# The idle products of TensorE's front: half as many, each over 256 columns instead of 128

## The chip, the cores and the metric

The kernel runs on one core of a Trainium2 chip. The metric is device time in microseconds (us), and a smaller one is better. The engines have short names in the profile: PE is TensorE's matrix products, PEld its loads of the stationary operand (they overlap the products), DVE is VectorE, ACT ScalarE, POOL GpSimd, and SP SyncE, which here issues DMAs. Each engine works through a queue of its own in program order. A product of 32-bit floats stands in the records as two passes, each with its own load, so that one matmul in the code is two PE and two PEld records.

## The reference

A gated linear recurrence over 768 steps for 4 x 8 heads of width 48, and behind it a feed-forward layer with a squared ReLU over 3072 tokens:

```python
for t in range(S):
    new_re = ar * S_re - ai * S_im          # ar, ai: a_re, a_im at step t, magnitude limited to 0.999
    new_im = ar * S_im + ai * S_re
    S_re, S_im = new_re + k[t] (x) v[t], new_im
    y[t] = einsum('bhd,bhde->bhe', q[t], S_re)
x = y as (B*S, H*D)                          # 3072 x 384
h = np.maximum(x @ w_in, 0.0)                # 384 x 2048
return h * h @ w_out                         # 2048 x 384
```

The idle products have no part in this: their result is read by nothing.

## The kernel before

The tokens are cut into 24 chunks of 128, taken two at a time as a group, and there are 12 groups. For each chunk the recurrence becomes products: DVE and ACT make operands from the gates (`make_operands`: squares, inverse roots, running products `totals`, `carries`, `carried`, then four `products` with queries and keys, and `heads_moved`, L990, which shifts some heads with a product on PE). `chunk` then holds the work on scores: `scores` (L1050, and L1033 for the state of the chunk before), `masked` (DVE), `sums_of_values` (L1087), `tokens` (ACT, L1099), `added` (L1112). The feed-forward part is `first_product` (L1179 for the chunks of the first two groups, one chunk at a time; L1195 for later groups, 256 tokens at a time), `squared_relu` on ACT, and the second product (L1215, and L1285 for most groups). `move_gaps` (L1169, L1170, and the ACT copy L1164) moves tokens between rows for the first chunk.

The weights come as 64-bit floats and are decoded in the kernel: a DMA brings a block as `words`, ACT makes two partial words (`low_part` L682, `high_part` L690) and DVE joins them (`decode`, L698). There are 16 such blocks. This decoding and the operands of the first groups fill DVE and ACT in the first 80 us, so TensorE has little to do there.

In that front TensorE runs idle products: `keep_busy` multiplies the identity `ident` with itself into a PSUM tile that nobody reads. The order of all work is written out by hand as a list of tokens, `FRONT`; each token `I<n>` calls `keep_busy(n)` once. The tokens I0 to I39 and I100 to I115 and two calls inside `scores` for the second chunk of the first group (L1040) make 58 calls. What they do:

```python
ident = const.tile([P, P], F32, name="ident")
idle = po.tile([P, DM], F32, tag="o", name="idle")[:, 0:P]
def keep_busy(n):
    for _ in range(2):
        nc.tensor.matmul(idle, lhsT=ident, rhs=ident, start=True, stop=True)
```

The idle products wait only for `ident` (POOL), and nothing waits for them but what stands behind them on PE's queue. In PE's order they stand at five places: 36 ahead of L630 (a transpose of the mask), 66 between L630 and the first L990, 2 inside the first chunk's block of scores work, 8 behind the first feed-forward products (L1179), and 4 inside the second chunk's scores.

## Time and profile before

| | before |
|---|---|
| median of 3 runs | 646.1 us (646.0 to 649.09) |
| the profiled execution | 644.23 us |
| its span, first to last instruction | 642.5 us |
| PE busy | 627.3 us, 98% of the span |
| DVE busy, ACT busy | 486.0 us (76%), 431.3 us (67%) |
| mean granted TensorE clock | 0.993 of full speed |

The span is 1.73 us shorter than the time of its own execution. PE is busy nearly throughout; where a change at the front is concerned, the questions are how early PE's unbroken work begins and whether it stays unbroken. The timeline rows give start and duration in us, engine, line, operation, output<-input, the number of instructions merged into the row, and in brackets the idle time before it with what ended it. A row's duration reaches to the modelled end of its last pass, so the pace of passes is read from one row's start to the next row's start.

### The profile page before, as it was taken

The numbers are of one execution on the slowest core, as the hardware profiler recorded it, in microseconds if no ns is written. First come the engines' busy times: TensorE is split into PE (matmuls) and PEld (weight loads), VectorE is DVE, ScalarE is ACT, GpSimd is POOL, SyncE is SP. The second block draws the span as 40 slices with busy tenths as digits, with TensorE's granted clock in tenths as the row PEclk, the third lists the DMA queues.
The fourth block names the chain that finished last, engine by engine and source line by source line (L and its number), as shares of the span: only waits on it lengthen the run. The fifth ranks groups of instructions, "written<-read, shape, count | busy, mean of one in ns | idle before, by whom it ended". The sixth has DMA issues, their size and how long they took to land.

```text
span 642.5 us, 16051 instructions
## 1 busy us (share of the span) xinstructions
PE 627.3 (98%) x6567; PEld 565.0 (88%) x6567; DVE 486.0 (76%) x975; ACT 431.3 (67%) x852; POOL 55.0 (9%) x124
## 2 busy tenths in 40 slices
PE   7989999999999999999999999999999999999996
PEld 7978878777899989999899999999989989999996
DVE  7969989978999865886888968878949859763130
ACT  5969989839696577685486577488587568544430
POOL 5430113001000011000110000100100011000000
PEclk9979999999999999999999999999999999999999
DMA  8996676071620723340731720823741741221201
GB/s 187 194 164 129 221 198 136 11 130 53 117 39 27 137 52 98 82 93 14 152 65 34 135 64 10 158 63 86 168 101 36 145 125 26 68 64 52 68 14 27
DMA packets 41494, 60.09 MB, mean 94 GB/s; under 512 B 5928, under 2 KB 29832, under 8 KB 41416
## 3 DMA queue, kind: packets, MB, share of 16 engines
q1 hardware_dynamic: 39240, 55.02, 39.2%
q0 software_dynamic: 1888, 3.69, 3.1%
q8 instruction: 52, 0.85, 0.6%
q10 hardware_dynamic: 288, 0.32, 0.2%
q14 instruction: 26, 0.21, 0.1%
HBM read 48.76 MB, written 4.72 MB: 83 GB/s over the span
## 4 chain that ended last, share of the span: by engine, by line
PE 94%; ACT 3%; DVE 1%; issue 1%; DMA 1%; POOL 0%; SPq 0%; ACTq 0%; POOLq 0%; DVEq 0%
PE h_ps L1195 32%; PE o_ps L1285 29%; PE o_ps L1215 6%; PE a_ps L1050 5%; PE h_ps L1179 5%; PE idle L579 4%; PE y L1033 3%; PE y L1087 3%; PE turns L1060 3%; PE turns L1112 3%; PE o_ps L990 1%; ACT part L682 1%; ACT part L690 1%; DMA last<-qk 1%; ACT h L1185 0%
## 5 line engine op out<-in xcount | busy, mean ns | idle before, releaser
L1195 PE MATMUL h_ps<-x,w 128*128 128x256 f32 x960 | 211.4, 379 | 0.0
L1195 PEld LDWEIGHTS h_ps<-x,w 128*128 128x128 f32 x960 | 181.4, 190 | 23.8
L1285 PE MATMUL o_ps<-w,h 128*128 128x192 f32 x640 | 109.8, 327 | 0.0
L1202 ACT ACTIVATE h<-h_ps 128x512 f32<-128x512 f32 x80 | 47.5, 594 | 86.2 <-PE h_ps L1195 86.0
L1285 PEld LDWEIGHTS o_ps<-w,h 128*128 128x128 f32 x640 | 103.9, 190 | 1.2 <-ACT o L1144 0.4
L499 DVE TENSOR_TENSOR pr<-ab 128x384 f32<-128x384 f32 (+3 forms) x196 | 70.7, 378 | 5.5 <-ACT ab L905 1.3
L1285 PE MATMUL o_ps<-w_sum,mix 128*128 128x192 f32 x320 | 55.2, 328 | 0.0
L499 DVE TENSOR_TENSOR ab<-pr 128x48 f32<-128x48 f32 (+3 forms) x210 | 50.1, 261 | 5.3
L1203 ACT ACTIVATE h<-h 128x512 f32<-128x512 f32 x80 | 50.5, 631 | 2.5
L1285 PEld LDWEIGHTS o_ps<-w_sum,mix 128*128 128x128 f32 x320 | 51.8, 190 | 0.3
L1179 PEld LDWEIGHTS h_ps<-x,w 128*128 128x128 f32 x384 | 45.9, 199 | 2.0 <-ACT x L1164 0.9
L1179 PE MATMUL h_ps<-x,w 128*128 128x128 f32 x384 | 47.0, 284 | 0.6 <-ACT x L1164 0.6
L499 DVE TENSOR_TENSOR qk<-ab,qk 128x768 f32<-128x768 f32 (+1 forms) x56 | 46.3, 847 | 1.2
L499 DVE TENSOR_TENSOR room<-ab,carry 128x1344 f32<-128x1344 f32 (+1 forms) x28 | 36.8, 1354 | 12.1 <-ACT carry L951 11.9
L1215 PE MATMUL o_ps<-w,h 128*128 128x384 f32 x128 | 44.2, 489 | 1.1 <-DVE w L698 1.1
L1099 ACT COPY x<-y 64x256 f32<-64x256 f32 (+1 forms) x72 | 26.6, 369 | 24.7 <-PE y L1087 23.5
L568 POOL COPY vt<-vt 64x192 f32<-64x192 f32 x48 | 23.2, 484 | 221.9 <-DMA vt<-in_vtok_dram 205.8
L1144 ACT ACTIVATE o<-o_ps 128x192 f32<-128x192 f32 (+1 forms) x44 | 15.0, 342 | 36.5 <-PE o_ps L1285 29.7
L824 ACT ACTIVATE ab<-raw 128x768 f32<-128x768 f32 (+1 forms) x28 | 38.0, 1379 | 0.1
L499 DVE TENSOR_TENSOR a<-a_ps,mask 128x768 f32<-128x768 f32 x24 | 22.9, 954 | 19.5 <-PE a_ps L1050 19.3
L1050 PE MATMUL a_ps<-qk 48*64 48x64 f32 (+1 forms) x1152 | 36.9, 244 | 0.0
L1050 PEld LDWEIGHTS a_ps<-qk 48*64 48x64 f32 x1152 | 35.7, 133 | 1.1 <-issue 0.7
(123 smaller groups left out, 982.0 us busy)
## 6 DMA issues: line engine op xcount, KB each, us to landing
raw<-in_feat_dram SPq DMA_DIRECT2D x40, 288.0 KB
words<-in_moe_w_out_dram SPq DMA_DIRECT2D x8, 768.0 KB
again<-in_moe_w_in_dram SPq DMA_DIRECT2D x16, 384.0 KB
again<-in_moe_w_out_dram SPq DMA_DIRECT2D x16, 384.0 KB
words<-in_moe_w_in_dram SPq DMA_DIRECT2D x8, 576.0 KB
vt<-in_vtok_dram SPq DMA_DIRECT2D x48, 96.0 KB
out_dram<-o SPq DMA_DIRECT2D x23, 192.0 KB
last<-qk SPq DMA_DIRECT2D x44, 97.5 KB
```

The lines of the kernel that those rows point to most:

```text
L499: nc.vector.tensor_tensor(out=out, in0=in0, in1=in1, op=op)
L568: nc.gpsimd.tensor_copy(out=v[half_rows(h), PAD + DM:PAD + DM + DM // 2].rearrange("t (a x) -> t a x", x=HH * D), in_=pairs[half_rows(1 - ...
L579: nc.tensor.matmul(idle, lhsT=ident, rhs=ident, start=True, stop=True)
L824: nc.scalar.activation(out=out.rearrange("p c j n -> p c n j"), func=AF.Copy, in_=in_.rearrange("p c (n j) -> p c n j", j=L), **kwargs)
L1050: nc.tensor.matmul(to[:, :, 2] if s else to[:, :, 0:2], lhsT=operand(2 + c, p_, rows(hh))[:, half_rows(s)], rhs=q_[:, :, 1] if s else q_, ...
L1099: nc.scalar.copy(out=x_of[gi][to, odd::2, b * C:(b + 1) * C], in_=tiles["y"][odd][of, 0:NP // 2])
L1179: nc.tensor.matmul(ps[:, j], lhsT=w1_blocks[:, k, g, at:at + P], rhs=x_of[i][:, g, b * C:(b + 1) * C], start=(g == 0), stop=(g == NG - 1))
L1195: nc.tensor.matmul(ps[:, j], lhsT=w1_blocks[:, k, g, at:at + P], rhs=x_of[i][:, g], start=(g == 0), stop=(g == NG - 1))
L1202: nc.scalar.activation(out=h, in_=h_ps[i, f], func=AF.Relu, scale=of_w1)
L1203: nc.scalar.activation(out=h, in_=h, func=AF.Square)
L1215: nc.tensor.matmul(o_of[i, b], lhsT=tokens_of(i, f, b)[:, j], rhs=w2[:, k], start=(k == 0), stop=(k == NFB - 1))
L1285: nc.tensor.matmul(to, lhsT=x(k)[:, j], rhs=factor(z)[:, 2 * k + j], start=(z in (0, 1, 3) and k == j == 0), stop=(k == KH // 2 - 1 and j ...
```

## The change

`keep_busy` issues one product in place of two. Its moving operand is the identity read twice (a broadcast over a new dimension of 2), 256 columns in place of 128, and the PSUM slice that it writes is twice as wide. The columns multiplied per call are the same; matmuls fall from 116 to 58, and each left out takes two loads and two passes with it. Nothing else is changed, and no other engine's order in this part of the kernel.

```diff
     ident = const.tile([P, P], F32, name="ident")
-    idle = po.tile([P, DM], F32, tag="o", name="idle")[:, 0:P]
+    idle = po.tile([P, DM], F32, tag="o", name="idle")[:, 0:2 * P]

     def keep_busy(n):
-        for _ in range(2):
-            nc.tensor.matmul(idle, lhsT=ident, rhs=ident, start=True, stop=True)
+        nc.tensor.matmul(idle, lhsT=ident, rhs=ident.unsqueeze(1).to_broadcast([P, 2, P]),
+                         start=True, stop=True)
```

On PE, at the start of the program (idle products, the mask's transpose L630, the first chunk's `heads_moved` L990 and the turned keys L1060):

```order
 L1537 BRANCH_PREFETCH_HINT
-L579 MATMUL idle<-ident 128x128 x36
+L578 MATMUL idle<-ident 128x256 x18
 L630 MATMUL turns<-ident,plain 128x64
-L579 MATMUL idle<-ident 128x128 x66
+L578 MATMUL idle<-ident 128x256 x33
 L990 MATMUL o_ps<-qk_119,o 128x260 x3
 L1060 MATMUL turns<-ident,qk_119 128x128 x3
```

Of 102 idle matmuls ahead of the first real ones 51 are left; all else keeps its place.

On PE behind the first chunk's scores, in the changed kernel (sums of values L1087, the products L1112 of `added`, then `move_gaps` L1169 and L1170):

```order
L578 MATMUL idle<-ident 128x256
L1060 MATMUL turns<-ident,qk_119 128x128 x3
L1087 MATMUL y<-a,vt_102 64x128 x4
L1087 MATMUL y<-a,vt_102 64x8x8 x4
L1087 MATMUL y<-a,vt_102 64x128 x4
L1087 MATMUL y<-a,vt_102 64x8x8 x4
L1112 MATMUL turns<-vt_102,kt_129 48x48 x8
L1112 MATMUL turns<-vt_102,kt_130 48x48 x8
L1169 MATMUL o_ps<-x,again 128x128
L1170 MATMUL o_ps<-x,o 128x128
```

Before, the first of these rows was two products over 128 columns; the rows behind it are the same, but 52 matmuls fewer stand ahead of L1112 than did before.

## Rows read from the trace of the kernel before

**Rows 1.** Busy time by stretch: us, then busy us (xrecords) of each engine, PEclk, DMA.

```profile
core 0: us, PE busy (x) PEld busy (x) DVE busy (x) ACT busy (x) POOL busy (x), PEclk, DMA share, GB/s
38.00:39.00 1.00, 0.00 (x0) 0.00 (x0) 0.96 (x2) 1.00 (x2) 0.80 (x2) 1.00 1.06 149
44.00:45.00 1.00, 1.00 (x7) 1.00 (x6) 0.00 (x0) 1.00 (x2) 0.55 (x1) 0.50 0.00 0
47.00:48.00 1.00, 1.00 (x12) 1.00 (x10) 0.00 (x0) 0.58 (x1) 0.66 (x2) 1.00 1.03 179
83.00:630.00 547.00, 546.98 (x5784) 491.11 (x5785) 414.24 (x777) 364.08 (x720) 29.62 (x68) 1.00 0.38 82
```

**Rows 2.** Timeline of PE, 14 to 56 us.

```profile
14.50 15.01 PE L579 MATMUL idle<-ident 128*128 128x128 f32 x132
29.34 1.48 PE L990 MATMUL o_ps<-qk,o 128*128 128x260 f32 x6
...
32.40 1.00 PE L1050 MATMUL a_ps<-qk 48*64 48x128 f32 x34
...
35.12 0.99 PE L1087 MATMUL y<-a,vt 64*64 64x128 f32 x32 [0.18 <-DVE a L499]
36.05 0.83 PE L1112 MATMUL turns<-vt,kt 128*48 128x48 f32 x26
39.01 0.38 PE L1112 MATMUL turns<-vt,kt 128*48 128x48 f32 x6 [2.14 <-issue]
39.32 0.49 PE L1169 MATMUL o_ps<-x,again 128*128 128x128 f32 x2
...
42.42 7.64 PE L1179 MATMUL h_ps<-x,w 128*128 128x128 f32 x48 [0.62 <-ACT x L1164]
...
52.59 3.17 PE L990 MATMUL o_ps<-qk,o 128*128 128x260 f32 x12 [0.75 <-DVE qk L499]
```

**Rows 3.** Timeline of PE, two rows of the later work.

```profile
163.70 18.29 PE L1195 MATMUL h_ps<-x,w 128*128 128x256 f32 x84
181.83 2.76 PE L1285 MATMUL o_ps<-w,h 128*128 128x192 f32 x16
```

**Rows 4.** Timeline of ACT, 38 to 49 us.

```profile
38.17 1.05 ACT L690 ACTIVATE part<-words 128x768 fp8e5<-128x768 uint8 x1
41.89 0.48 ACT L1164 COPY x<-o_ps 128x384 f32<-128x384 f32 x1 [2.67 <-PE o_ps L1170]
...
44.06 1.05 ACT L690 ACTIVATE part<-words 128x768 fp8e5<-128x768 uint8 x1
47.42 0.60 ACT L1185 ACTIVATE h<-h_ps 128x512 f32<-128x512 f32 x1 [2.30 <-PE h_ps L1179]
...
48.58 0.25 ACT L951 COPY carry<-ab 128x90 f32<-128x90 f32 x1
```

**Rows 5.** Timeline of DVE, 27 to 50 us.

```profile
27.41 1.02 DVE L499 TENSOR_TENSOR qk<-ab,qk 128x384 f32<-128x384 f32 x2
...
34.11 0.96 DVE L499 TENSOR_TENSOR a<-a_ps,mask 128x768 f32<-128x768 f32 x1 [0.40 <-PE a_ps L1050]
...
45.15 0.96 DVE L698 SCALAR_TENSOR_TENSOR w<-words,part 128x768 int32<-128x768 int32 x1 [2.06 <-ACT part L690]
48.86 1.63 DVE L499 TENSOR_TENSOR room<-ab,carry 128x672 f32<-128x672 f32 x2 [2.75 <-ACT carry L951]
```

**Rows 6.** DMA queue of instructions: whole run; begun in 20.3:20.4; 35.7:35.8; 42.1:42.2.

```profile
q8 instruction: 52, 0.85, 0.6%
...
q8 instruction: 1, 0.02, 85.9%
...
q8 instruction: 1, 0.02, 94.6%
...
q8 instruction: 1, 0.02, 94.1%
```

**Rows 7.** The chain of work that ended last, in order of time: start, us, what.

```profile
79.34 3.64 DMA last<-qk
```

## The prediction

> **What bounds the kernel now.** I read the busy time by stretch first. From 83 us to 630 us PE is idle for 0.02 us in all [rows 1]: TensorE sets the time there, so whatever moves the start of that stretch moves the end by as much. What is ahead of 83 us is a chain through PE, ACT and DVE, which the chain of waits ends with a DMA (`last<-qk`, 3.64 us from 79.34) for which PE waits [rows 7]. So the question is what the change does between 3 and 83 us.

> I read PE's timeline there next. The idle products are on the path only where real work behind them on PE's queue is already waiting. At 29.34 it is: the first L990 reads two products of DVE that were finished at 27.41 + 1.02 = 28.43 [rows 2, 5]; PE reached it 0.9 us later because of 132 idle passes. The 8 calls behind L1179 end before DVE has the operands of the next L990, which PE then waits 0.75 us for [rows 2]: they are covered.

> The third thing to see is a hole. PE stops in the middle of L1112, after 26 of its 32 passes, for 2.14 us, with nothing named but "issue" [rows 2]. These products read tiles that the first 26 passes of the same block read too. What it costs can be followed: ACT waits 2.67 us for L1170, then 2.30 us for L1179; DVE waits 2.06 us for ACT's L690, then 2.75 us for ACT's L951 [rows 4, 5]. [...]

> **What the hole is.** The instruction queue q8 moved 52 packets of 0.85 MB, 16 KB each [rows 6]. The page counts 6567 products and as many loads on PE: 13,134 records, 253 for a packet, so q8 brings PE's code in blocks of about 256 records (an estimate; other control instructions fill the rest). Counting matmuls in PE's order (four records each), the hole comes after 178 matmuls (36 + 1 + 66 + 3 + 3 + 3 + 32 + 2 + 3 + 16 + 13), 712 records. One block, 64 matmuls, earlier is after 114, the start of the first scores; one more is after 50. PE passes the earliest at about 14.50 + 13 x 0.225 = 17.4 us, the next just behind the start of L1050, at about 32.5 [rows 2], and the third is the hole, left at 39.01. The packets begin at 20.3, 35.7 and 42.1 [rows 6]: 2.9, 3.2 and 3.1 us behind. The second took 0.946 x 16 engines x 0.1 us = 1.51 us, so it ended at about 37.25 in the middle of the hole, and PE went on 1.76 us after that. I read this so: a block is asked for when PE passes into the one before it, is there some 6.5 us later, and PE ran through the 256 records of scores and sums of values in less than that. Ahead of the first two boundaries were slow idle products, which gave the first packet time.

> **The change, part by part.** The sum is made against the profiled execution, 644.23 us, of which 642.5 is span and 1.73 lies outside; the median of the runs is 1.87 above it, and I add that at the end.

> (a) Pace. 132 narrow passes took 29.34 - 14.50 = 14.84 us, 112.4 ns each; wide ones, 84 passes of L1195, 18.13 us, 215.8 ns [rows 2, 3]. A wide pass replaces two narrow ones (224.8): 9 ns less. The 66 calls save 0.59 us; the first 36, partly at half clock, between 0 and 0.32. I take 0.7. L990 has 0.9 us of room, so it starts 0.7 earlier. DVE's mask step behind it waited only 0.40 us for PE [rows 5], so DVE, and with it L1087, gain 0.4. A broadcast operand of these strides doesn't occur in the trace; the pace of L1195 is the nearest row, and the 4 wide ones in the second scores are worth 0.04 us at most.

> (b) The hole. 52 matmuls leave ahead of L1112 (18 + 33 + 1), 208 records. The boundary after 114 matmuls now lies after the first matmul of L1112, and the one after 178 lies 9 matmuls into the second chunk's scores, at about 56 us on the old scale. The boundary after 50 lies in the idle stretch, 31 wide calls in, at 14.2 + 31 x 0.432 = 27.6 us. Its packet should begin near 30.6, end near 32.1 and serve PE from 33.9; PE needs it at L1112, at 36.05 - 0.4 = 35.65. There is 1.8 us of room. The next one is asked for there, is ready by 42, and needed after 50. The hole goes.

> (c) What is late next. ACT's copy L1164 stands behind L690, which ended at 38.17 + 1.05 = 39.22, now 38.8; the 12 passes of L1169 and L1170 need 12 x 112 ns = 1.35 us at full clock and start by 36.9, so they are done by 38.4. ACT sets it: L1164 at 38.8 in place of 41.89, 3.1 us earlier. Then the first 24 passes of L1179 (half of the 48 of that row) take 24 x 112 ns + 0.16 = 2.85 us in place of the 5.00 from 42.42 to L1185's start: ready at 42.2. ACT's other work between L1164 and L1185 takes 3.22 us and ends at 42.05. L1185 starts at 42.2 in place of 47.42, 5.2 us earlier. Then L951 comes at 43.4 and DVE, whose wait for L690 also shrinks, starts `carried` at about 43.7 in place of 48.86: **5.2 us**.

> (d) From there to 83 us. The next L990 waits for DVE [rows 2], which moves whole. Loads are issued behind steps that move too, and in 44 to 45 us the DMA engines did nothing [rows 1], so they have room to move. I let 0.2 us get lost to loads and keep **5.0 us**. Bounds: 3.0 if half the gain of (c) is lost again, 5.2 if nothing is. From 83 us PE is unbroken and hands all of it on: 644.23 - 5.0 = 639.2, and with 1.87 for the median **641.1 us**.

> [...]

> **The rivals.** *The hole stays.* If it belongs to L1112 and not to a block of code, the same 2.14 us follow, and only (a) is left: 0.4 us, 645.7. For it: no row names what ended it. Against it: it lies in mid-block, and the packet's time fits [rows 2, 6].

> *The clock falls all the same.* PE still works thinly between 33 and 40 us, with products of 48 and 64 columns. If the clock is 0.50 there as before, L1169 to L1170 keep their 2.5 us and the first half of L1179 its 5.0: L1164 at 39.4, that half done at 44.9 in place of 47.4, a gain of 2.5 us: 643.6. Against it: the 2.14 us of no work just ahead of the fall are gone.

> *The code comes late: slower.* The boundary now lies at the first matmul of L1112, not at its fourteenth. If the packet ends as late as 37.25, as before, PE is served at 39.0 and does all of L1112 after that, 1.2 us in place of 0.4: 0.8 us later than before, at half clock behind it: 646.9. It decides at a packet end of 36.4, 4.3 us later than I reckon. For it: the DMA engines are full (1.06 in 38 to 39 us) [rows 1].

> *The clock doesn't rise on wide idle products.* At half clock the 33 calls would take twice 14.2 us and L990 would start some 13 us late: 659. Against it: the stretch of L1195's wide passes ran at 1.00 [rows 1, 3].

> **How the numbers follow.** Forecast (hole gone, clock held) 0.55; clock falls all the same 0.15; hole stays 0.18; code late 0.09; clock doesn't rise 0.03. The likeliest gives 641.1. The range, 8 in 10: from 640.0 (5.2 us, and some scatter; the runs of before lie 646.0 to 649.09) to 646.2, which takes in the first three cases. A measurement of this kernel can tell some 0.5%, 3.2 us, from no change: faster than 642.9 is the forecast with nearly all its weight and a little of the second case, 0.55; within 0.5% are the second to fourth, 0.40; slower 0.05.

> **What would show it.** Right: no "issue" hole in L1112, and none elsewhere of over 0.5 us; the first q8 packet near 30.6 in place of 20.3; PEclk 1.00 between 38 and 48; L1164 near 38.8, L1185 near 42.2, `carried` near 43.7; idle passes at 216 ns; PE unbroken from some 78 us on. Wrong: a hole at L1112's first matmul or in the second scores, PEclk 0.50 in 40 to 47, or loads that ACT waits for between 44 and 58, which would take back what (c) gives.

## The result and the profile after

| | before | after |
|---|---|---|
| median of 4 runs each | 646.78 us (646.0 to 649.09) | 639.72 us (638.63 to 641.11) |
| ratio | | 0.9886 (0.9853 to 0.9919) |
| the profiled execution | 644.23 us | 639.79 us |
| its span | 642.5 us | 638.1 us |

The change makes the kernel faster by 1.1%. That is 0.28 us below the low end of the range on record. The two profiled executions lie 4.44 us apart, the medians 7.06: where the difference of 2.6 us comes from is the main thing that the prediction got wrong.

Busy time by stretch of the kernel after (columns as in [rows 1]); the first two stretches are shown of before too, the third begins at 79 us in place of 83:

```profile
core 0: us, PE busy (x) PEld busy (x) DVE busy (x) ACT busy (x) POOL busy (x), PEclk, DMA share, GB/s
38.00:39.00 1.00, 1.00 (x11) 0.91 (x8) 0.93 (x4) 0.98 (x2) 0.96 (x3) 1.00 1.15 231
44.00:45.00 1.00, 1.00 (x11) 1.00 (x11) 1.00 (x3) 0.97 (x3) 0.95 (x2) 1.00 1.08 214
...
79.00:630.00 551.00, 550.86 (x5798) 494.90 (x5791) 415.33 (x780) 364.51 (x720) 30.35 (x68) 1.00 0.38 81
```

In 38 to 39 us PE does 11 passes, where it did none. In 44 to 45 us the granted clock is 1.00, where it was 0.50, and PE does 11 passes in place of 7. From 79 us PE is busy throughout, but for 0.14 us.

PE's timeline (columns as in [rows 2]):

```profile
13.71 14.51 PE L578 MATMUL idle<-ident 128*128 128x256 f32 x66
30.14 1.55 PE L990 MATMUL o_ps<-qk,o 128*128 128x260 f32 x6 [1.92 <-DVE qk L499]
...
36.24 1.00 PE L1087 MATMUL y<-a,vt 64*64 64x128 f32 x32
37.16 0.93 PE L1112 MATMUL turns<-vt,kt 128*48 128x48 f32 x32
38.02 0.49 PE L1169 MATMUL o_ps<-x,again 128*128 128x128 f32 x2
...
40.72 5.62 PE L1179 MATMUL h_ps<-x,w 128*128 128x128 f32 x48 [0.95 <-ACT x L1164]
46.18 1.89 PE L578 MATMUL idle<-ident 128*128 128x256 f32 x8
48.88 3.17 PE L990 MATMUL o_ps<-qk,o 128*128 128x260 f32 x12 [0.81 <-DVE qk L499]
```

L1112's 32 passes are one unbroken row of 0.93 us; the "issue" hole of 2.14 us in [rows 2] is gone. L1179's 48 passes take 5.62 us in place of 7.64, at full clock. What is new is the wait of 1.92 us ahead of the first L990. DVE and ACT, which wait for these products:

```profile
28.98 1.02 DVE L499 TENSOR_TENSOR qk<-ab,qk 128x384 f32<-128x384 f32 x2
...
45.15 1.63 DVE L499 TENSOR_TENSOR room<-ab,carry 128x672 f32<-128x672 f32 x2
```

```profile
40.21 0.46 ACT L1164 COPY x<-o_ps 128x384 f32<-128x384 f32 x1
...
43.70 0.60 ACT L1185 ACTIVATE h<-h_ps 128x512 f32<-128x512 f32 x1 [0.25 <-PE h_ps L1179]
...
44.87 0.25 ACT L951 COPY carry<-ab 128x90 f32<-128x90 f32 x1
```

DVE's products for the first L990 begin 1.57 us later than in [rows 5] (28.98 against 27.41). Nothing of the change is ahead of them on DVE; these first operands come at another time in each execution, as the runs below show. All the same ACT's L1185 is 3.72 us earlier than in [rows 4] and `carried` on DVE 3.71 us earlier than in [rows 5]. ACT's waits of 2.67 and 2.30 us are down to none and 0.25.

The instruction queue over the whole run, for packets begun in 24.4 to 24.5 us, and in 40.2 to 40.4 us (queue, kind: packets, MB, share of 16 engines), and the DMA of the chain of waits that answers to [rows 7] (start, us):

```profile
q8 instruction: 51, 0.84, 0.6%
...
q8 instruction: 1, 0.02, 85.8%
...
q8 instruction: 1, 0.02, 46.0%
```

```profile
75.57 2.71 DMA last<-qk
```

One packet fewer, as the 232 records left out let one expect (12,902 products and loads to 51 packets are 253 each, as before). The first two packets are at 24.5 and 40.3 us in place of 20.3 and 35.7, so none is on its way while TensorE runs through the scores.

### The profile page after: what moved, and what is told of

Its sections match the earlier page's. It is cut to its first block, busy times and chain, and to the rows that moved or that the text cites. A ratio compares the mean times of both kernels' runs of the same rounds, so it can differ in the third digit from the quotient of the medians.

```text
span 638.1 us, 15819 instructions
## 1 busy us (share of the span) xinstructions
PE 623.6 (98%) x6451; PEld 556.5 (87%) x6451; DVE 486.0 (76%) x975; ACT 431.3 (68%) x852; POOL 57.0 (9%) x124
## 3 DMA queue, kind: packets, MB, share of 16 engines
HBM read 48.76 MB, written 4.72 MB: 84 GB/s over the span
## 4 chain that ended last, share of the span: by engine, by line
PE 85%; DVE 5%; ACT 4%; DMA 3%; issue 1%; POOL 1%; SPq 0%; ACTq 0%; DVEq 0%; POOLq 0%
PE h_ps L1195 32%; PE o_ps L1285 28%; PE o_ps L1215 6%; PE a_ps L1050 4%; PE h_ps L1179 4%; PE y L1087 3%; PE y L1033 3%; DMA raw<-in_feat_dram 3%; PE turns L1060 2%; PE turns L1112 2%; ACT part L682 1%; DVE room L499 1%; DVE ab L499 1%; DVE qk L499 1%; ACT part L690 1%
## 5 line engine op out<-in xcount | busy, mean ns | idle before, releaser
L1195 PE MATMUL h_ps<-x,w 128*128 128x256 f32 x960 | 211.4, 379 | 0.0
L1195 PEld LDWEIGHTS h_ps<-x,w 128*128 128x128 f32 x960 | 181.4, 190 | 23.8
L1179 PE MATMUL h_ps<-x,w 128*128 128x128 f32 x384 | 44.9, 276 | 1.0 <-ACT x L1164 1.0
L1179 PEld LDWEIGHTS h_ps<-x,w 128*128 128x128 f32 x384 | 43.9, 192 | 2.2 <-ACT x L1164 1.1
L568 POOL COPY vt<-vt 64x192 f32<-64x192 f32 x48 | 25.2, 525 | 218.5 <-DMA vt<-in_vtok_dram 168.5
L1144 ACT ACTIVATE o<-o_ps 128x192 f32<-128x192 f32 (+1 forms) x44 | 14.9, 341 | 36.4 <-PE o_ps L1285 29.0
L1050 PE MATMUL a_ps<-qk 48*64 48x64 f32 (+1 forms) x1152 | 36.9, 244 | 0.0
L1050 PEld LDWEIGHTS a_ps<-qk 48*64 48x64 f32 x1152 | 35.7, 133 | 1.3 <-issue 1.0
L824 ACT ACTIVATE room<-z 128x768 f32<-128x768 f32 (+1 forms) x27 | 36.5, 1408 | 0.1
```

Source lines behind the costliest of these rows:

```text
L568: nc.gpsimd.tensor_copy(out=v[half_rows(h), PAD + DM:PAD + DM + DM // 2].rearrange("t (a x) -> t a x", x=HH * D), in_=pairs[half_rows(1 - ...
L824: nc.scalar.activation(out=out.rearrange("p c j n -> p c n j"), func=AF.Copy, in_=in_.rearrange("p c (n j) -> p c n j", j=L), **kwargs)
L1050: nc.tensor.matmul(to[:, :, 2] if s else to[:, :, 0:2], lhsT=operand(2 + c, p_, rows(hh))[:, half_rows(s)], rhs=q_[:, :, 1] if s else q_, ...
L1179: nc.tensor.matmul(ps[:, j], lhsT=w1_blocks[:, k, g, at:at + P], rhs=x_of[i][:, g, b * C:(b + 1) * C], start=(g == 0), stop=(g == NG - 1))
L1195: nc.tensor.matmul(ps[:, j], lhsT=w1_blocks[:, k, g, at:at + P], rhs=x_of[i][:, g], start=(g == 0), stop=(g == NG - 1))
```

## The experiments

**The kernel before once more.** No edit.

> The kernel before, unchanged, to see how its executions spread. Theory (the hole in L1112 and the half clock behind it cost more in most executions than in the profiled one): the executions spread over 644 to 649 us, and the mean granted clock of an execution goes with its time, lower clock with longer time; from the profiled one (0.993, 644.2) a further stretch at half clock of 3.4 us would show as about 0.990 and some 2 us more. Rival (the difference lies outside the front): the clock is 0.993 in all of them and the time spreads without it.

645.07 us; ratio 1.0017 (0.9983 to 1.005). PE's timeline:

```profile
29.77 1.55 PE L990 MATMUL o_ps<-qk,o 128*128 128x260 f32 x6 [0.59 <-DVE qk L499]
...
36.79 0.83 PE L1112 MATMUL turns<-vt,kt 128*48 128x48 f32 x26
40.27 0.38 PE L1112 MATMUL turns<-vt,kt 128*48 128x48 f32 x6 [2.66 <-issue]
```

The hole is at the same pass with another length. In this execution the clock held at 40 us and fell later, from 83.5 to 86.9 us. In the first profiled execution of before it had fallen at 39.8 us, 0.8 behind the hole's end. So a fall did not always follow the hole at once. Over the ten executions a lower mean clock goes with a longer time, as the theory on record had it, from 643.32 us at 0.997 to 647.47 us at 0.989.

**Six small products more.**

```diff
+        for _ in range(6 if len(calls) == 20 else 0):
+            nc.tensor.matmul(idle[0:32, 0:16], lhsT=ident[:, 0:32], rhs=ident[:, 0:16], ...)
         for _ in range(2):
             nc.tensor.matmul(idle, lhsT=ident, rhs=ident, start=True, stop=True)
```

> The kernel before with six more matmuls of 32x16 among the idle ones (24 more records, under 1 us of TensorE's time, all covered or nearly). Theory (the hole is TensorE out of code at a block's boundary): the hole moves with the count, from behind the 26th pass of L1112 to behind its 14th, and ends at the same time or later, so it is 2.0 to 3.0 us long; time as before within 1 us. Rival (the hole belongs to L1112 itself): it stays behind the 26th pass, 2.1 us.

639.18 us (638.01 to 640.04); ratio 0.9911 (0.9886 to 0.9937).

```profile
37.52 0.56 PE L1118 MATMUL turns<-vt,kt 128*48 128x48 f32 x14
38.38 0.65 PE L1118 MATMUL turns<-vt,kt 128*48 128x48 f32 x18 [0.30 <-issue]
```

The hole moved from pass 26 to pass 14, 6 matmuls earlier, as foretold. But it is 0.30 us long, and more work gives nearly all that the change gives. The mean clock was 0.998 or more in all ten runs. The place was right, the length and the time were wrong; why is told under "The race".

**Wide products, with the records of before.** 17 of the wide calls behind L630 became 68 small products.

```diff
+        if 19 <= len(calls) <= 35:
+            for _ in range(4):
+                nc.tensor.matmul(idle[0:32, 0:16], ...)
+            return
```

> The changed kernel, but 17 of the 33 wide idle products ahead of the first L990 are replaced by 68 matmuls of 32x16, so that about as many matmuls stand ahead of L1112 as in the kernel before (one fewer). Theory (code): the hole is back, behind the 28th pass of L1112, 1.5 to 2.5 us, and the time is back at the kernel before, ratio 0.997 to 1.002. Rival (wide products as such, their pace or their fewer weight loads, make the gain): no hole, ratio 0.988 to 0.992 as for the changed kernel.

641.06 us; ratio 0.9954 (0.9924 to 0.9983). There is an "issue" hole behind pass 28, as foretold, but of 0.22 us, and the time lies between what the two theories said:

```profile
39.68 0.83 PE L1120 MATMUL turns<-vt,kt 128*48 128x48 f32 x28
40.74 0.29 PE L1120 MATMUL turns<-vt,kt 128*48 128x48 f32 x4 [0.22 <-issue]
```

The small products ended early; TensorE then waited 4.68 us for DVE, the clock fell to 0.50 from 28.85 to 35.67 us, and it reached the boundary 3.6 us later than in before. So the run was made again in another form: 62 small products in place of the first 10 wide calls, so that the idle stretch ends with wide ones.

```diff
+        if 19 <= len(calls) <= 28:
+            for _ in range(7 if len(calls) <= 20 else 6):
+                nc.tensor.matmul(idle[0:32, 0:16], ...)
+            return
```

> The changed kernel with 10 of its wide calls (the first 10 behind the mask's transpose) replaced by 62 products of 32 x 16: net 52 more, so that PE has as many records ahead of L1112 as before, while the idle stretch stays as long (62 took some 4.1 us by the pace of the run with 68, 10 wide ones 4.3) and ends with 23 wide calls. If the count decides: the boundary lies behind pass 26 of L1112 again, PE resumes 1.6 to 1.8 us behind the end of the packet, and the median is 641.5 to 645 us with a spread of over 3 us. If the width of the products decides: no hole there and 639.5 to 640 us, as the changed kernel.

640.85 us; ratio 0.994 (0.9912 to 0.9968).

```profile
30.70 2.94 PE L998 MATMUL o_ps<-qk,o 128*128 128x260 f32 x6 [3.27 <-DVE qk L499]
...
39.05 0.83 PE L1120 MATMUL turns<-vt,kt 128*48 128x48 f32 x26
40.22 0.38 PE L1120 MATMUL turns<-vt,kt 128*48 128x48 f32 x6 [0.34 <-issue]
```

With 52 matmuls put back the hole is behind pass 26 again, products wide or not. The time fell between what the two theories said, and the profiled execution again waited for DVE (3.27 us) and reached L1112 3 us late.

**The change in the first 18 calls only.** The rest stay narrow, so the records ahead of L1112 are 72 fewer, not 208.

```diff
+        if len(calls) <= 18:
+            nc.tensor.matmul(idle, lhsT=ident, rhs=ident.unsqueeze(1).to_broadcast([P, 2, P]), ...)
+            return
         ...                                # the two narrow products of before
```

> The change in the first 18 calls alone (the 36 products ahead of L630); the other 40 calls keep two products over 128 columns. 18 matmuls fewer. Theory (code): the boundary moves from L1112 to the tenth matmul of L1179, which TensorE reaches after the block has come; no hole, clock 1.00 from 38 to 48 us, nearly the whole gain of the change, ratio 0.986 to 0.992. Rival (pace of the wide products makes the gain): a third of the wide products gives a third of the gain or less, ratio 0.996 to 1.000.

640.01 us; ratio 0.9942 (0.992 to 0.9965), just above the 0.986 to 0.992 that was foretold. No hole; L1112 is one row of 32 passes. The boundary lies in L1179 at 41.3 us; its packet had ended at 39.4. So the change in 18 of the 58 calls takes the hole away. The changed kernel was not run on this chip, so what the 40 calls that stayed narrow cost is not shown.

**The race.** In every kernel with an "issue" hole in this stretch it stood ahead of the 705th record of PE in the trace: 349 passes, 349 loads and 6 records of PE's sequencer come before (the first record, at 0.32 us, is not counted). The prediction counted 712, because it took the transposes L630 and L1060 at four records each, and they have two. I set beside it when the 449th was passed (256 earlier, by the estimated length of a block), what TensorE needed from there to the 705th without the hole, and q8's second packet. All are us of the profiled executions:

| kernel | at record 449 | its way to 705 | packet | hole | resumes behind the packet's end |
|---|---|---|---|---|---|
| before | 32.41 | 4.46 | 35.74 to 37.25 | 2.14 | 1.76 |
| before, again | 33.14 | 4.48 | 37.24 to 38.56 | 2.66 | 1.71 |
| six small more | 31.68 | 6.41 | 35.17 to 36.75 | 0.30 | 1.63 |
| wide, 68 small | 36.05 | 4.47 | 37.73 to 39.03 | 0.22 | 1.71 |
| wide, 62 small first | 35.40 | 4.48 | 37.11 to 38.57 | 0.34 | 1.65 |
| first 18 wide | 32.93 | 8.39 | 37.84 to 39.38 | none | |

So the hole is the packet's start behind record 449, plus the packet (1.3 to 1.6 us), plus 1.6 to 1.8 us, less TensorE's way. That sum only says again what the columns mean; what is found is that the last term is nearly the same in all five executions with a hole, and that the place is a count. With six matmuls more ahead of it, the block begins six matmuls earlier too, and these are L1060's three and the second three of L990 (260 columns), which take some 1.9 us; the six that fall out behind are L1112's short ones. The expectation had left out what the block holds. Three runs that this foretells:

**A slower block, same count.** The two products of the call inside the first chunk's work got 384 columns.

```diff
-            nc.tensor.matmul(idle, lhsT=ident, rhs=ident, ...)
+            if len(calls) == 52:
+                nc.tensor.matmul(idle, lhsT=ident, rhs=ident.unsqueeze(1).to_broadcast([P, 3, P]), ...)
```

> The kernel before with the two idle products of the call inside the first chunk's work (between scores and turned keys) widened from 128 to 384 columns. No count changes, so the boundary stays behind pass 26 of L1112; but TensorE needs some 0.85 us longer for the 256 records ahead of it (4 passes of about 324 ns in place of 112), 5.3 us where both traces of before have 4.47. If the hole is a race between the packet and TensorE's way through the block, the hole is 0.6 to 0.9 us shorter than before's 2.1 to 2.7, TensorE resumes 1.6 to 1.8 us behind the packet's end all the same, and the time is at or a little under that of before, 642 to 644.5 us. If the hole has a length of its own, it stays over 2 us and the time is 0.7 us above before.

642.8 us (641.26 to 647.78); ratio 0.9992 (0.9959 to 1.0024).

```profile
34.61 1.56 PE L583 MATMUL idle<-ident 128*128 128x384 f32 x4
...
37.25 0.83 PE L1119 MATMUL turns<-vt,kt 128*48 128x48 f32 x26
38.91 0.38 PE L1119 MATMUL turns<-vt,kt 128*48 128x48 f32 x6 [0.83 <-issue]
```

The way is 5.00 us, the packet ended at 37.16, and PE went on 1.74 us behind it. The hole shrank by 1.3 to 1.8 us, more than foretold, since this packet began 2.58 us behind record 449 and not 3.3 to 4.1. The median is that of before within the interval.

**Thirteen small products more.** The boundary lies at the first pass of L1112.

```diff
-        for _ in range(6 if len(calls) == 20 else 0):
+        for _ in range(13 if len(calls) == 20 else 0):
```

> The kernel before with 13 products of 32 x 16 added in the 20th call (0.9 us in the idle stretch). The boundary moves to the first pass of L1112, and the one ahead of it from the start of L1050 back into the last idle products, so that the block between them now holds all six wide products of L990 (260 columns): 6.9 us or more of work where before has 4.47 and the kernel with 6 added has 6.27. By the race this leaves no hole, or under 0.3 us, and 638.3 to 640 us. If what counts is only how early in L1112 the boundary lies (the rival on record, code that comes late), TensorE stops ahead of the whole of L1112 and the time is 644 to 647 us.

640.06 us (638.91 to 641.13); ratio 0.993 (0.9901 to 0.9959).

```profile
37.53 0.93 PE L1118 MATMUL turns<-vt,kt 128*48 128x48 f32 x32
```

The time is just above the 638.3 to 640 us that was foretold. No hole, with a way of 8.39 us, though the boundary lies earlier in L1112 than anywhere else. This is the place where I had priced the rival "code comes late". The packet began at 29.47 us, 0.33 behind record 449.

**Two calls fewer.** 4 narrow products less.

```diff
+        if len(calls) in (20, 21):
+            return
```

> The kernel before with two calls (4 narrow products, 0.9 us) left out in the idle stretch and nothing else. The boundary moves 4 matmuls later, behind the first product of L1169, and the block ahead of it takes some 4.75 us. By the race the hole is there, 1.5 to 2.5 us, now in front of L1170, and the time is that of before, 642.5 to 645.5 us. If the gain of the change comes from fewer or shorter idle products, this has part of it: 641.5 us or less and no hole.

642.9 us (641.29 to 648.09); ratio 0.9998 (0.9968 to 1.0029).

```profile
30.34 2.94 PE L995 MATMUL o_ps<-qk,o 128*128 128x260 f32 x6 [3.02 <-DVE qk L499]
...
38.67 0.93 PE L1117 MATMUL turns<-vt,kt 128*48 128x48 f32 x32
39.53 0.49 PE L1174 MATMUL o_ps<-x,again 128*128 128x128 f32 x2
41.06 0.49 PE L1175 MATMUL o_ps<-x,o 128*128 128x128 f32 x2 [1.04 <-issue]
```

The hole went where the count puts it, between L1174 and L1175 (L1169 and L1170 of before). It is shorter than the 1.5 us or more that was foretold: its packet began 2.65 us behind record 449, and the way is 4.72 us. The time did not change. In this execution TensorE also stood for 3.02 us ahead of the first product of L995, and the clock was 0.50 from 30.09 to 33.50 us, so the time holds that loss too. It shows that two calls fewer did not bring the gain, and no more.

**What the hole's length and the clock cost apart.** The kernel after was run again, and with a pause as long as the hole behind pass 26 of the first L1112: once 5 wide products, once 33 small ones.

```diff
                         nc.tensor.matmul(add[rows(hh), c, p_], lhsT=kt[c][:, p_, hh], ...)
+                        if gi == 0 and b == 0 and (c, p_, hh) == (IM, 2, 0):
+                            for _ in range(5):
+                                keep_busy(0)
```

In the quiet form the last two lines are `for _ in range(33):` and a product of 32 x 16.

> The changed kernel once more, beside the kernel before on one chip, to size the term that failed: I had carried the 1.87 us between the profiled execution of before and its median over to the changed kernel. If that distance belonged to the hole and the half clock that some executions of before have, the median here is 639 to 640 us and the runs lie within 2.5 us of each other, while those of before spread over 4 us or more. If it was the first result that came out low by chance, the median is 641 or more and the spread is that of before.

> The changed kernel with 5 wide idle calls (5 x 432 ns = 2.16 us) put behind pass 26 of the first chunk's L1112: a pause as long as the hole, in which TensorE is busy. The boundary of code moves only from 9 to 4 matmuls into the second scores. It prices the length of the hole alone: ACT's L1164 has 0.4 us of room, so 1.5 to 2.2 us more than the changed kernel, 641.2 to 641.9 us, with the clock at 1.00. If the hole's length is hidden and only the slow products behind it cost, it is within 0.5 us of the changed kernel.

> The same pause with 33 products of 32 x 16 (66 passes at 33 ns = 2.18 us) in place of the 5 wide ones. The boundary of code then lies behind 10 matmuls of L1179, some 45 us, and its packet should be there by 43.5. If a quiet stretch of this length lets the clock fall: PEclk 0.50 for several us from about 40 on in the profile or in many executions (a mean clock of 0.99 to 0.996), and 1 to 4 us more than with the busy pause, 642.5 to 645.5 us. If the fall in the kernel before had another cause than the hole: the same time and clock as with the busy pause.

| kernel | median | clock 0.998 or more | clock below 0.998 |
|---|---|---|---|
| after | 638.15 us; ratio 0.9923 (0.9895 to 0.9951) | 8 runs, 638.11 | 1 run, 642.22 |
| busy pause | 641.93 us; 0.9971 (0.9948 to 0.9994) | 9 runs, 641.86 | 1 run, 644.29 |
| quiet pause | 641.87 us; 0.9961 (0.9935 to 0.9988) | 5 runs, 640.87 | 5 runs, 642.96 |

Of the kernel after eight of nine runs lie within 2.0 us (637.82 to 639.82); with the ninth the spread is 4.4 us, more than the 2.5 that was foretold. PE's row of the pause and ACT's copy behind it, of the busy pause, and then PE's row of the quiet one:

```profile
36.40 2.43 PE L578 MATMUL idle<-ident 128*128 128x256 f32 x10
```

```profile
40.76 0.48 ACT L1167 COPY x<-o_ps 128x384 f32<-128x384 f32 x1 [1.94 <-PE o_ps L1173]
```

```profile
37.17 2.26 PE L1116 MATMUL idle<-ident 128*32 128x16 f32 x66
```

The busy pause of 2.16 us moved ACT's copy by 2.29 us against the kernel after (38.47 below). In medians it cost 3.8 us where I had foretold at most 2.2; 0.6 us of it is a later wait for a load (`last<-qk` at 277 us), and about 1 us I can't name. So the hole's length is not hidden. In the median the quiet pause costs as much as the busy one, and less than the 642.5 us that was foretold if the clock falls. But with it the mean clock was below 0.998 in 5 runs of 10, against 1 of 10 and 1 of 9, and those five took 2.1 us more than the other five. Over the other kernels it is alike: with a hole of at most 0.30 us and a wait of under 2 us for the first L990 (the kernel after, six and thirteen small, first 18 wide) the clock was below 0.998 in 3 runs of 43, in the kernel before in 67 of 91. So a stretch of 2 us with little or no work goes with a lower mean clock in many runs here, not in all. The trace of the quiet pause's profiled execution has no fall, so where the falls of the five lie is not shown.

**Half the idle work, with the changed kernel's count.** One narrow product in each call.

```diff
-        for _ in range(2):
-            nc.tensor.matmul(idle, lhsT=ident, rhs=ident, start=True, stop=True)
+        nc.tensor.matmul(idle, lhsT=ident, rhs=ident, start=True, stop=True)
```

> The kernel before with one narrow product in each call in place of two: the changed kernel's count of records in every place, and half of its idle work. The boundaries are those of the changed kernel, so no hole in the scores. But the idle stretch ends near 21 us and TensorE stands still for some 7 us until L990's operands are there. If such a stretch lets the clock fall as in the two kernels that ended it 3 to 4.7 us early (mean clock 0.993 to 0.996, 640.9 and 641.1 us), most executions are at 640.5 to 642.5 us; if the count is all that matters here, 638 to 640 us as the changed kernel.

640.59 us; ratio 0.9946 (0.9918 to 0.9975); one execution of 3559 us is left aside. PE's first L990 and two stretches:

```profile
28.69 2.94 PE L989 MATMUL o_ps<-qk,o 128*128 128x260 f32 x6 [6.20 <-DVE qk L499]
```

```profile
22.00:27.00 5.00, 0.50 (x5) 0.31 (x3) 4.68 (x7) 4.67 (x9) 2.02 (x4) 1.00 1.02 197
28.00:33.00 5.00, 4.31 (x12) 3.46 (x13) 4.82 (x10) 3.33 (x6) 3.14 (x6) 0.50 0.83 189
```

No hole, but TensorE stands for 6.20 us, and behind that the clock is 0.50; the mean clock was 0.988 to 0.992 in all nine executions. The time is within what was foretold for a clock that falls (640.5 to 642.5 us). So the count alone took away the hole here, and the width made the idle stretch longer (to 28.2 us in the changed kernel, 22.5 here): there the wait was 1.92 and 0.69 us in the two profiled executions, and the clock behind it 1.00.

## Why the prediction was wrong, and what of it held

**The step that failed: "and with 1.87 for the median".** The sum's own time, 639.2 us, fits: the profiled executions of the changed kernel took 639.79 and 638.15. The prediction then added the distance between before's profiled execution and the median of its three runs, as if it were a constant that the changed kernel has too. The runs showed none: the changed kernel's median lies 0.07 us below its profiled execution in the result (639.72 beside 639.79) and on it in the second measurement (638.15). For the kernel before itself it did not hold either. Its 91 runs beside the experiments have their median at 644.29 us, 0.06 above the profiled 644.23; only 25 of the 91 are as long as the shortest of the result's four, 646.0. Whether chance or the chip made those four so long, no run shows.

What the term took for a constant is scatter. The 91 runs by mean granted clock: 24 runs at 0.998 or more, median 642.27 us; 34 at 0.995 to 0.997, 644.06; 33 below, 646.93. Of the changed kernel's 13 runs 11 are at 0.998 or more. Without the 1.87 the forecast would have been 0.5 us from the result's median (1.1 from the second one), and the range's low end some 638. It was to be seen beforehand: three runs over 3.1 us, all above the one execution whose trace has the hole and the half clock, give no distance that may be handed on to a kernel that is to have neither.

That 639.79 comes so near to the 639.2 of the sum is in part luck: DVE's operands were late in that execution, and (d) was too small, as told below.

**The hole is code and goes.** Right: the hole followed the count of records through five edits, and TensorE resumed 1.6 to 1.9 us behind the packet's end each time. What I read wrongly is the packet's start. I put it 2.9 to 3.2 us behind the boundary before; over all runs the second packet began 0.3 to 4.9 us behind it, and the first from 2.1 us ahead to 6.3 behind (in the changed kernel 24.48 us, while record 193 was passed at 26.12). So in the changed kernel the first packet began at 24.5 us and not at 30.6, with more room than reckoned. That some packets began ahead of the boundary speaks against "a block is asked for when PE passes into the one before it", as far as the start goes; that PE stopped ahead of the 705th record and went on 1.6 to 1.9 us behind a packet's end is what the runs show. With a way of 7.7 us (the quiet pause) or more TensorE did not stop there; with ways of 4.5 to 6.4 us it stood for 0.2 to 2.7 us. What else a block holds beside the 253 products and loads for a packet is not shown.

**The clock holds.** Right: 1.00 from 7.9 to 635.9 us in the changed kernel's trace, so the rival "falls all the same" didn't come; in that of before it was 0.50 from 39.8 to 46.7 us. A lower mean clock, 0.996, is in 2 of the changed kernel's 13 runs (641.11 and 642.22 us); where the clock fell in them is not shown.

**(a) Pace.** The 66 passes took 14.51 us where 132 took 15.01: 0.50 saved, 0.59 reckoned; from start to start a wide pass took 217 ns, 216 foretold. It gave nothing, since L990 then waited for DVE (1.92 and 0.69 us). The time of DVE's first operands differs by up to 2.3 us from one execution to the next (27.23 to 29.54), which I had taken as fixed. The first idle passes were slower in both kernels: 213 ns a narrow one up to 9.1 us, 427 a wide one up to 7.9, where later ones took 112 and 216.

**(c) and (d).** The profiled execution of the result lost 1.57 us to those operands, so its steps are late by that: 40.21, 43.70 and 45.15 for 38.8, 42.2 and 43.7. In the kernel's second profiled execution DVE was early (27.23). ACT's and then DVE's rows there:

```profile
38.47 0.45 ACT L1164 COPY x<-o_ps 128x384 f32<-128x384 f32 x1
...
41.95 0.60 ACT L1185 ACTIVATE h<-h_ps 128x512 f32<-128x512 f32 x1 [0.26 <-PE h_ps L1179]
```

```profile
43.40 1.63 DVE L499 TENSOR_TENSOR room<-ab,carry 128x672 f32<-128x672 f32 x2
```

Each is 0.25 to 0.35 us ahead of what I reckoned: `carried` gained 5.46 us, 5.2 by the sum. Of (d) the sign was wrong: the loads took nothing back there. The next DMA of [rows 7] began at 73.80 us there, 5.54 earlier, and took 2.86 us in place of 3.64; the span is 6.1 us shorter, where I let 5.0 stand.

**How the gain divides.** Before's runs at full clock (642.27 us) lie 4.2 us above the changed kernel's (638.11): that is the hole's own length of 2.1 to 2.7 us with what follows from it. The busy pause cost 3.8 us, near to that, though some 1 us of its cost has no name. Before's median of 91 runs (644.29) lies another 2.0 us higher, and the runs of a lower mean clock (644.06 and 646.93) make that difference: this part goes with the falls of the clock.

## What to carry to other kernels

An "issue" hole in mid-block on an engine that is fed by many short instructions can be its code, as the one ahead of record 705 was here: count the records between holes and packets of the instruction queue (253 products and loads for a packet here), and look at the time that the engine takes for the 256 records ahead, the estimated length of a block here: holes came with 4.5 to 6.4 us, and none with 7.7 us or more. Then a few instructions more, ahead of it, can be as good as many fewer: six small products more gave 639.18 us here and 58 products fewer 639.72, since the six moved the boundary to a block with longer ones, for which TensorE needs 6.41 us in place of 4.46. And a distance between one profiled execution and the median of a few runs is no constant: ask which event in the trace makes it, whether the change removes that event, and whether more runs still show it.

## What the runs showed of the hardware that I had not expected

- Six products of 16 columns more, 0.5 us of work, made the kernel 5 us faster in the median (639.18 against 644.25 us): the hole stood behind pass 14 and not 26, and was 0.30 us long and not 2.14.
- In the kernels with a hole the packet of code of 16 KB (0.85 MB in 52 packets) took 1.25 to 1.6 us (DMA share 1.16 and 1.03 in 36 to 38 us of before), and TensorE went on only 1.6 to 1.9 us behind its end.
- The packet's start was no fixed time behind the boundary (2.1 us ahead to 6.3 behind); what sets it was not tried and stays open.
- In the profiled executions the clock fell to 0.50 each time that TensorE waited for the first L990 for 3.02, 3.27, 4.68 or 6.20 us, and not where it waited 1.92 us or less there. Behind the hole it fell 0.8 us after the hole's end in one execution of before, and in the other only 43 us later.
